# Gated mix of a spectral filter and a Mish MLP: the order of the input loads, and a new written-out order of all engine queues

## The chip, the cores and the metric

The kernel runs on 1 core of one Trainium2 chip. The metric is the device time of one execution in microseconds (us), the slowest core's, as a median over runs. The profile shows one execution, with times counted from its first instruction.

## The reference, cut to what matters

```python
x = A_x                                                   # [1, 2048, 512] bf16
g = sigmoid((x * gate_w).sum(-1, keepdims=True))
# A: 2-D real FFT over tokens and features, times a complex weight, back
X = rfft2(x.astype(f32), axes=(-2, -1)) * (w_r + 1j * w_i)   # w: [2048, 257]
a = irfft2(X, s=(2048, 512)).astype(bf16)
# B: MLP with Mish, F = 1792
h = einsum("bsd,df->bsf", x, w1) + b1
act = h * tanh(log1p(exp(-abs(h))) + max(h, 0))
b = einsum("bsf,fd->bsd", act, w2)
return g * a + (1 - g) * b
```

Both branches read the same x. Branch A is a chain of small matmuls against constant tables with two passes through memory in between; branch B is two large matmuls.

## The kernel before, in words

Tokens are tiled as 16 tiles t of 128 partitions (token = 16 * partition + t); features are 4 slices of 128, the 1792 hidden units 14 slices "ft". B handles the tokens in 4 chunks c of 512.

**Names of the tasks.** Each piece of work is a named task, and the names below are used throughout.

- Loads, all but a few on the queue of SyncE (SP): `ld_x0` to `ld_x12` (x by groups of tiles, lines 433 to 435), `ld_w1_lo_h` (w1 by ranges of ft and halves of the features, 437 to 441), `ld_fm`, `ld_gm`, `ld_rf`, `ld_ri` (tables of the transforms), `ld_gw`, `ld_b1`, `ld_Wp..`, `ld_Wm..`, `ld_Wz.` (18 loads of the spectral weight W, 458 to 463), `ld_w2_0`, `ld_w2_1`.
- x transposed: tiles 0 to 7 through TensorE (`tr`, line 481) and copied out of PSUM (`evx`, 409/410); tiles 8 to 15 by VectorE in 32 x 32 blocks (`tp8` to `tp15`, line 489) and then by 16 shuffle DMAs (`sh`, line 495), half of them on SP's queue and half on GpSimd's. A shuffle waits for all eight `tp`.
- B: `mm1_c_ft` (line 795, four matmuls of 512 columns), `mish_c_ft` on ScalarE (811), `mm2_t_part` (830, seven matmuls of 512 columns), `bev_t` (776/777, scaled by 1 - g into xo).
- A, forward: `ts`, `td` (sums and differences, VectorE, 414), `a10_t`, `a11_t` (533), `eg_t` (ScalarE, 540), `e1p`, `e1m`, `e1f` (VectorE, 414, 549/550), `s1_t` (559), `e2_t` (564), `r1w` (scratch written: 16 DMAs on SP, 568) and `r1r0` to `r1r3` (scratch read back, 640).
- A, spectrum, in four groups v: `s2_u` (656), on VectorE `wm` (times W, 414, PSUM to Qb), on GpSimd `wz` (414, Qb to Zb), the small chain `cv`, `crv`, `rcc`, `cv2`, `cm`, `chs`, `wc` for one column, then `s2i_v` (716), `e4` (copies out), `r2w_v` (scratch written, 726), and after all four `r2r0` to `r2r3` (731). Before the first product stand `wcols`, `rcw`, `weff`, `wab1`, `wab2`, which need all 18 loads of W.
- A, inverse, by tile: `s1i_t` (744), `e5_t`, `a1i_t` (755), `gc_t` (ScalarE, 760), `sam_t`, `sap_t` (VectorE, 766), `sbm_t`, `sbp_t` (GpSimd, 414; for tiles 14 and 15 also on VectorE), then `sum_t` (VectorE, 414, 850) and the stores `out`; tiles 14 and 15 end in `fin` (842).
- Gate: `gdot` (16 on VectorE, 575), `gpow` (GpSimd, 580), `gadd`, `gcol`, `omg` (582 to 585).

**The order.** It is not found at build time. A string `ORDER` lists every task of the program in one sequence: two digits (base 62) are the number of the task in the order in which the code adds them, then comes the engine where there is a choice, and the PSUM bank where the task opens one.

```python
for _ in tasks:                                            # lines 230 to 251, shortened
    t = tasks[digit(2)]
    if t.opts:
        t.eng, t.dur, t.fn = next(o[:3] for o in t.opts if o[0] == ENGINE[ORDER[pos]])
    for p in t.alloc or ():
        b0 = digit(1)
        ...                                                # waits for the last users of the bank
    order[t.eng].append(t)
```

Each engine runs its own list strictly in this order and waits, in front of a task, for what the task reads, for the buffer it overwrites and for its bank. A wait holds everything behind it on that engine; SP's list holds DMA issues alone. The loads themselves are added here:

```python
433  def ld_x(t0, t1):
434      dma(f"ld_x{t0}", xo[:, t0:t1, :], xv[:, t0:t1, :], ...)
...
451  ld_x(8, 12)
452  ld_w1(8, 14, ("sp", "sp"))
453  ld_x(12, 16)
```

**SP's list of before, decoded:** ld_x0, x2, fm, w1_4_0, x4, x8, w1_8_0, w1_8_1, x12, gm, gw, Wp00; eight `sh`; w2_1 and nine loads of W; r1w0b; Wm01, w2_0, Wp13, Wp11; then `r1w` with Wp03 and Wm11 among them; Wp01, Wm13, rf; r1r0, r1r3, r1r1, r1r2; ri; r2w0 to 3; r2r0 to 3; the stores. GpSimd's list has `ld_b1` and the other eight `sh`.

**VectorE's list of before** in the front: evx0a, 0b, 2a, 2b, ts0, td0, ev_small, e1m_2, evx6, tp10, tp9, evx4, tp11, 8, 13, 14, 15, 12, ts1, e1p_2, e1p_0, td1, e1m_0, then `gdot` among `e1`; the last nine `gdot` behind e2_12, gadd, gcol, omg, weff, then wm01, cv_1, wm00.

Of the kernel before, what the change touches and what calls it, by code (L numbers as in the profile page):

```python
# [257 lines left out]
ORDER = (
    "0M04005060P070208090A000B0Q0C010R0D0E0F0G0H0T0I0x60J0N0yv0K0z50L7510V0O7F211610v13312v7K47A714v767L0S7M770U787"
    "B0W7C1Zv7G1X0037H1av1l50X1b61n1m33J0Y1Y0Z1pv7D7P00a17518v1d1B791A7T67U15116v1C191E7R51c60b1F1G7I7Q1D7N1Q7f01N1"  # L260
    "vv7J7h11V7b21ov1ev1wv7O1U1S7V41W7g7c8307E7S8J21fv1J1M8977i1P8H534283332718K1O1T1L36841y20v1x01gv0g0j1K7W381z0i"
    "8L41I0l8D68701R8M7z4297x18820v2Bv1H2Av8A21v350c2Iv2Ca2Hv7X02Jv8E22a7d32fv2D60s807y0f7Y0p2iv2gv7e2Kv1h10o2L41qv"
    "8l02N1iv0k2M32Ea1k8B48510e2Pv0u2V22W60q8n70m2hv8C2F2Ov8m2X861j0h2Yv2Zv1r30n1sa2Qa8b02312k62j32G8F42av8I24v262t"
    "52l1u2u38o2b12v2mv2nv1t2xv8177v52ca2R125822d2wv2ya2z68G372oa2e8p32Sv7w2p4392qv3A7Z130a8t68r22U3C8N73E8Z47a318u"
    "8h52T3B8q8a2r8c3G8x33D3F2s320d8j13H3I0r3K3L0t8k3T7s68f48O3O7t3W3P03M3N3Q8s8i3U3X18g3R8Pa3hv3S3Y47j77p07ua3a7q3"
    "gv3lv8d63kv3jg8y3Z3b7k8e7rv3t23ig3u43ng43v3V3v4F07la7m63mg8z74H903w42v47v3x46v7n3c79P24Ov4G37oa44g3y63d9X50w45"
    "g49g3e9Q4I4Sv9Y8v23z8w4J8Q748g4Pv4Tv4K28R4L403f3o3p34b08Sv8T23rv4M419T74A3qa9U8U4B34N4d4Rg8Va3s4kv4Qg4lv4Da4c0"
    "4Vg4W9V74Ca4e4Ug4mg4pv4f9W4E8W24ov4ng4g44h4i9N34qg4X49F04j4Za9114Yv9O4rg4s4t4924uv4va4a9Z49D38X9459G9J64w9L79E"
    "9M9709a8Ya93a954x5915H35Aa5P751496v5Qa9b29K5R55S4y9c5v15f75n65Iv5J352v5U5K5B4985T5wa4z5325C5M5L5oa5D5Wg5Vg5E5x"
    "55Ng5gv5y605Og9R15z5p350545X699a9H45Ya6R75q5Fg566J65Gg5h09S6Ka556Sv62gA1v5r9d56B16T29e61g5s5i9A76x66L36U5k6Ca6"  # L270
    "V6D55ug5Z15j6309I6EA8v58g57g5a5tgA2v6M5mg6p46W9B9yv5lg6N6Yg6ya6qa6h26ia6O9f66z2A7v5c6G5b706Xg5dg64aA5v719i45eg"
    "650A36Z36Pg6F6r59l1669Ca6Ig6j79zv6s9g6Qg6aa6b39j9m729p267689s0AEv6k6HgA4v6Ag74v6u6c6t9v5A96l69g6mA06wvA6ABv6d9"
    "ka6eAAv6vv6ogAC9haADv6ng9nAHv6fg73g6ggAF9o9qAGv9rAI9t9w9u9x"
)
# [17 lines left out]
def _build(nc, A_x, A_w_r, A_w_i, B_x, B_w1, B_b1, B_w2, gate_w, out):  # L292
# [8 lines left out]
    with es:  # L301
# [76 lines left out]
        def dma(name, dst, src, reads=(), writes=(), nbytes=0, deps=(), is_out=False, prio=None, queue="sp", bw=380e3, tail=1.1, nd=128, issue=0.62):  # L378
            t = G.add(name, queue, issue if issue != 0.62 or queue != "pool" else 1.0, lambda e: e.dma_start(dst, src),  # L379
                      reads=reads, writes=writes, lat=tail, deps=deps, prio=prio)  # L380
# [584 lines left out]
```

## Time and profile before

| what | value |
|---|---|
| runs, median (lowest to highest of 3) | 131.43 us (130.37 to 131.91) |
| the profiled execution's own time | 131.48 us |
| its span, first to last instruction | 129.7 us |
| busy: TensorE / VectorE / ScalarE / GpSimd | 123.0 / 91.6 / 69.4 / 56.3 us |
| granted TensorE clock | 1.00 |

A row of the timeline gives the start, the busy time of the merged instructions, engine, line, operation, out<-in, their count, and in brackets the idle time before them with what ended it. "PE" is TensorE, "PEld" its weight loads, "DVE" VectorE, "ACT" ScalarE, "POOL" GpSimd; a "q" behind it is the engine's sequencer, which issues DMAs. A busy time of several pipelined matmuls runs over into the next row by some 0.16 us.

### The profile page before, as it was taken

The numbers are of one execution on the slowest core, as the hardware profiler recorded it, in microseconds if no ns is written. First come the engines' busy times: TensorE is split into PE (matmuls) and PEld (weight loads), VectorE is DVE, ScalarE is ACT, GpSimd is POOL, SyncE is SP. The second block draws the span as 40 slices with busy tenths as digits, with TensorE's granted clock in tenths as the row PEclk, the third lists the DMA queues.
The fourth block names the chain that finished last, engine by engine and source line by source line (L and its number), as shares of the span: only waits on it lengthen the run. The fifth ranks groups of instructions, "written<-read, shape, count | busy, mean of one in ns | idle before, by whom it ended". The sixth has DMA issues, their size and how long they took to land.

```text
span 129.7 us, 2726 instructions
## 1 busy us (share of the span) xinstructions
PE 123.0 (95%) x1014; PEld 66.1 (51%) x1014; DVE 91.6 (71%) x178; ACT 69.4 (54%) x119; POOL 56.3 (43%) x90
## 2 busy tenths in 40 slices
PE   7999999999999999699999999999999999999960
PEld 5776546445554444344444444444447666555650
DVE  0456999898699981179499795541006997999992
ACT  1306777798997537500336047454077988674300
POOL 4000047000000009146879499930000799979770
PEclk9999999999999999999999999999999999999999
DMA  3999618799998667991000032555089000224045
GB/s 88 337 402 394 199 40 219 216 263 189 289 314 242 197 173 223 331 390 43 0 5 3 0 93 73 162 162 159 13 285 356 3 5 3 81 81 157 10 152 172
DMA packets 19293, 21.16 MB, mean 163 GB/s; under 512 B 1744, under 2 KB 15952, under 8 KB 19152
## 3 DMA queue, kind: packets, MB, share of 16 engines
q1 hardware_dynamic: 18176, 19.67, 48.6%
q10 hardware_dynamic: 816, 0.79, 1.9%
q0 software_dynamic: 288, 0.53, 1.5%
q8 instruction: 8, 0.13, 0.4%
q14 instruction: 5, 0.04, 0.1%
HBM read 13.64 MB, written 6.29 MB: 154 GB/s over the span
## 4 chain that ended last, share of the span: by engine, by line
PE 85%; DMA 5%; DVE 3%; POOL 2%; issue 1%; POOLq 1%; DVEq 0%
PE ps L795 37%; PE ps L830 29%; DMA Abuf<-scr 5%; PE ps L744 3%; PE ps L755 3%; PE ps L533 3%; PE ps L559 3%; PE ps L430 3%; POOL Tg L414 2%; PE ps L656 2%; PE ps L716 2%; DVE Qb L766 1%; PE ps L481 1%; DVE xo L842 1%; DVE xT L409 1%
## 5 line engine op out<-in xcount | busy, mean ns | idle before, releaser
L795 PE MATMUL ps<-xT,w_sb 128*128 128x512 bf16 (+1 forms) x240 | 53.8, 365 | 0.3 <-DVE xT L409 0.3
L830 PE MATMUL ps<-w_sb,act 128*128 128x512 bf16 (+2 forms) x252 | 52.2, 355 | 0.0
L811 ACT ACTIVATE act<-ps,b1f 128x512 bf16<-128x512 f32 x56 | 36.5, 687 | 26.6 <-PE ps L795 26.6
L830 PEld LDWEIGHTS ps<-w_sb,act 128*128 128x128 bf16 x252 | 22.8, 98 | 23.0 <-issue 0.6
L795 PEld LDWEIGHTS ps<-xT,w_sb 128*128 128x128 bf16 x240 | 22.3, 98 | 21.9 <-DVE xT L409 0.8
L414 POOL TENSOR_TENSOR Tg<-Qb 128x256 bf16<-128x256 f32 x29 | 22.6, 812 | 17.4 <-DVE Qb L766 17.4
L414 POOL TENSOR_TENSOR Zb<-Qb 128x510 bf16<-128x510 f32 x16 | 20.0, 1268 | 3.2 <-DVE Qb L414 2.6
L414 DVE TENSOR_TENSOR Qb<-ps,WT 128x1024 f32<-128x1024 f32 x16 | 18.9, 1215 | 3.4 <-PE ps L656 3.3
L766 DVE SCALAR_TENSOR_TENSOR Qb<-ps,gcol,Qb 128x256 f32<-128x256 f32 x32 | 13.6, 473 | 1.5 <-issue 0.8
L580 POOL TENSOR_TENSOR gcol<-omg,gdot 128x16 f32<-128x16 f32 x1 | 2.9, 2942 | 26.6 <-DVE Tg L575 26.6
L410 ACT ACTIVATE Ybuf<-ps 128x1024 bf16<-128x1024 f32 x9 | 9.1, 1024 | 6.5 <-PE ps L716 6.2
L414 DVE TENSOR_TENSOR Abuf<-ps,Tg 128x512 bf16<-128x512 f32 x16 | 10.4, 685 | 2.7 <-ACT Tg L540 1.5
L409 DVE CAST Ybuf<-ps 128x1024 bf16<-128x1024 f32 x7 | 8.6, 1223 | 3.8 <-PE ps L716 3.1
L379 POOL DMA_DIRECT2D xT<-act x8 | 4.0, 503 | 15.5 <-DVE act L489 15.5
L575 DVE SCALAR_TENSOR_TENSOR Tg<-xo,Tg 128x512 bf16<-128x512 bf16 x16 | 10.5, 685 | 0.2
L776 ACT ACTIVATE xo<-ps,omg 128x512 bf16<-128x512 f32 x11 | 7.3, 687 | 5.2 <-PE ps L830 3.5
L777 DVE TENSOR_SCALAR xo<-ps,omg 128x512 bf16<-128x512 f32 x3 | 2.3, 751 | 10.8 <-PE ps L830 10.8
L760 ACT ACTIVATE Qb<-ps,gcol 128x256 f32<-128x256 f32 x16 | 7.1, 473 | 4.3 <-PE ps L755 4.2
L414 DVE TENSOR_TENSOR xo<-xo,Tg 128x512 bf16<-128x512 bf16 x14 | 9.0, 653 | 0.0
L540 ACT ACTIVATE Tg<-ps 128x512 f32<-128x512 f32 x8 | 4.7, 594 | 6.2 <-PE ps L533 6.2
L410 ACT ACTIVATE Zb<-ps 128x512 bf16<-128x512 f32 x12 | 7.0, 603 | 1.0 <-PE ps L744 1.0
L409 DVE COPY xT<-ps 128x512 bf16<-128x512 bf16 (+1 forms) x6 | 2.9, 505 | 5.7 <-PE ps L481 5.7
(61 smaller groups left out, 88.1 us busy)
## 6 DMA issues: line engine op xcount, KB each, us to landing
Abuf<-scr SPq DMA_DIRECT2D x8, 512.0 KB, 6.8
scr<-Ybuf SPq DMA_DIRECT2D x16, 128.0 KB, 2.2
scr<-Ybuf SPq DMA_DIRECT2D x4, 512.0 KB, 2.9
w_sb<-in_B_w_dram SPq DMA_DIRECT2D x2, 896.0 KB, 6.6
out_dram<-xo SPq DMA_DIRECT2D x7, 256.0 KB, 2.0
xo<-in_A_x_dram SPq DMA_DIRECT2D x3, 512.0 KB, 7.5
rt<-c_rt SPq DMA_DIRECT2D x2, 512.0 KB, 7.4
WT<-in_A_w_r_dram SPq DMA_DIRECT2D x7, 128.5 KB, 5.6
```

Of the source, the lines that this page charges most:

```text
L379: t = G.add(name, queue, issue if issue != 0.62 or queue != "pool" else 1.0, lambda e: e.dma_start(dst, src), reads=reads, writes=writes, ...
L409: fs = {"dve": ("dve", dve_dur(n, rate=rate), lambda e: e.tensor_copy(out=dst(), in_=src())), "act": ("act", act_dur(n), lambda e: e.activ ...
L410: "act": ("act", act_dur(n), lambda e: e.activation(dst(), src(), AF.Copy))}
L414: f = lambda e: e.tensor_tensor(out=o(), in0=i0(), in1=i1(), op=op)
L540: G.add(f"eg_{t}", "act", act_dur(512), lambda e, gb=gb, pa=pas[0], pv=pv: e.activation(G0[:, gb].rearrange("p t c (m s) -> p t c m s", s= ...
L575: lambda e, t=t: e.scalar_tensor_tensor(out=junk[t % 2], in0=xo[:, t, :], scalar=1.0, in1=gwb, op0=ALU.mult, op1=ALU.mult, accum_out=gdot[ ...
L760: lambda e, t=t, sl=sl, p5=p5: e.activation(gC[:, sl, :].rearrange("p (i n) -> p i n", i=2), ps[:, p5.bank, :].rearrange("p (i n) -> p i n ...
L766: lambda e, t=t, sl=sl, p5=p5, o=o, op=op: e.scalar_tensor_tensor(out=st1[:, sl, o::2, :], in0=ps[:, p5.bank, :].rearrange("p (i n) -> p i ...
L776: G.add_multi(f"bev_{t}", [("act", act_dur(512, True), lambda e: e.activation(xo[:, t, :], ps[:, pd.bank, :], AF.Copy, scale=omg[:, t:t + ...
L795: ins = e.matmul(o if c < 2 else o.rearrange("p (a t j) -> p a t j", a=4, t=4), w1_sb[:, i, 128 * ft:128 * (ft + 1)], xTp[:, i, 512 * c + ...
L811: lambda e, c=c, ft=ft, pd=pd, hb=hb: e.activation(act[:, hb, ft, :].rearrange("p (t a j) -> p t a j", t=4, a=4), ps[:, pd.bank, :].rearra ...
L830: ins = e.matmul(ps[:, pd.bank, cs_], act[:, hb, ft, 128 * tl:128 * (tl + 1)], w2_sb[:, ft, cs_], start=(ft == 0), stop=(ft == NFT - 1))
```

## The change

Two lines of the loads change places, so x's tiles 12 to 15 are issued in front of w1's last slices (ft 8 to 13), and the string `ORDER` is replaced as a whole. No task is added or removed; 23 copies, scalings and sums change their engine (21 between ScalarE and VectorE, in both directions, and two between GpSimd and VectorE), and many tasks change their PSUM bank.

```diff
@@ -256,21 +256,21 @@
 ORDER = (
-    "0M04005060P070208090A000B0Q0C010R0D0E0F0G0H0T0I0x60J0N0yv0K0z50L7510V0O7F211610v13312v7K47A714v767L0S7M770U787"
...
+    "0M0N0420506070P080O090A0B0U0C00010Q0D0R0E020F0G0H0I0x00yv0J0K0L0T0z30S10v037F27511151347A314v1X67K70V7B12a1Y7G"
...
@@ -449,8 +449,8 @@
         ld_x(8, 12)
+        ld_x(12, 16)
         ld_w1(8, 14, ("sp", "sp"))
-        ld_x(12, 16)
```

What the new string says, decoded:

| list | new order, where it differs |
|---|---|
| SP | ld_x0, x2, fm, w1_4_0, x4, x8, **x12, w1_8_0, w1_8_1**, Wp00, **Wm00**, gw, gm; eight `sh`; Wp01, Wm10, **w2_1**, Wz0, Wm13, Wz1, Wm11, Wm12, Wm02, Wm03, **w2_0**, Wp11, Wp12, Wp03; r1w0b, Wp13, Wp10, then the other fifteen `r1w` without a load among them; Wp02, Wm01, rf; r1r and all behind it as before, the stores in another order |
| GpSimd | ld_b1 first; then ones, ident, ebz; the eight `sh`; ebase behind them. Then wz01, **wz00**, crv_0, wz11, **cm_0, chs_0**, wz10, **wc0**, ... and the `sb` in the order 2, 0, 1, 3, 4, 5, 6, 7, ... 12, 13, 14 |
| VectorE | evx0a, 0b, 2b (**evx2a on ScalarE**), ts0, td0, ev_small, e1m_2, **e1p_2, evx4, evx6, tp8, 9, 10, 13, 15, 12, 11, 14**, ts1, td1, gdot0, ...; the last eight `gdot` behind e2_12, then **weff, gadd, cv_0, wm01, gcol, wm00, wm10, omg**, bev_3, cv_1, wm11, cv2_0, ... |
| TensorE, to the first `s2` | both lists have the same length of work in front; rcw stands one `mm2` half earlier |
| TensorE, first `s2` to first `s1i` | 15 `mm2` halves and 15 `mm1` (before: 17 and 13); up to s2i_3 10 and 10 (before: 12 and 9), behind it 5 and 5 (before: 5 and 4) |
| TensorE, behind the first `s1i` | 11 `mm2` halves and 2 `mm1` (before: 9 and 4), then tile 15 as before; behind the last `a1i` three `mm2` halves (before: two) and tile 15 |

Of the 18 loads of W one stood in front of the shuffles before and two do now; the inverse table (`ld_ri`) stands behind the shuffles, and behind r1r2, in both lists.

More of the change, by code (lines that the diff above doesn't have):

```diff
@@ L258 @@
 ORDER = (
-    "0M04005060P070208090A000B0Q0C010R0D0E0F0G0H0T0I0x60J0N0yv0K0z50L7510V0O7F211610v13312v7K47A714v767L0S7M770U787"
[L260 to L273, printed above, removed]
+    "0M0N0420506070P080O090A0B0U0C00010Q0D0R0E020F0G0H0I0x00yv0J0K0L0T0z30S10v037F27511151347A314v1X67K70V7B12a1Y7G"
@@ new lines @@
+    "7C7L0W7M7H761Zv1av7D1l41m01n7I0X7R51c60Y7E1547J1pv1ov173777T216v7818v0b0c7S191A7V00a791B1b31E1G8350Z7U1D1C1d1F"
+    "7v41vv7N1M1V1K8L17P27O1T7w1L1wv1H7W893337f71W2741N1O1fv348F07Q841R8G1U1qa0d8D236292857g381ev2Av7b03A8J47c1P8M0"
+    "l7x71x61y07h10v1J8K1z1Q1gv2Bv351S1I20v0j21v2Cv2iv0r8B47y2fv0s8H52Hv8E7i2Iv2Jv8A2D08l61h20n0p2Ea2L72V07d18I2Kv8"
+    "m2gv1r50g2N2X0i1iv0u0m22v0o0h2M22hv1sa8C2W38578702351k2Pv2u42Yv0q2Zv0k7e2t32Ov1j1t2k124v2G2aa2j2861u2F7z72b52v"
+    "2wv2xv2l2Qa88252R22ca8n0802ya8d4262e2z52nv2Sv2U2mv3C8e2oa8Z7372p22T2qv2d30a3J8a7X17Z68r731328j48x58t23E2s7Y398"
@@ new lines @@
+    "f38u8p18y7a8b28o3B3G2r0f7s50e3D7j08s8c7t3I3F0t3H3K3O8h63P77k3Q3R8k3S8q3L3T3Y18g3X33W3Z3U3hv8i3M3gv7p73kv8v67q3"
+    "jg8133N7uv8w3ig823a7m47la3b3lv3V3c63ng3t24F03d3e3u542v0w3f3mg7n3o3v7ra43v45g3w8N746v8O7oa3x44g47v48g3y249g3p33"
+    "z4H4Ov9Z28Pa8Q73ra4Pv4Qg4G03qa4b34Tv4I4Rg9a9R54J9D69N29S404d9E4K54Sv9X08R4lv414L4A4kv4c54Ug9O9Y4Vg4e4B04M8Sa4C"
+    "a4N9P44f4pv8W74W4ov8z54g64mg4ng4Da4X04h8T64rg3s904Zv4qg4i4j9J54s4Ya4t04E9Q4ua8U4vv4a9H49V09T19F28Va943959K9W9I"
+    "9d68X4w4x96a9U9e9154y9G5905135H45Ia4z505P29L65J15Aa5n45K5Qv52v5M5L5R25oa5B09M8Yv533925X45C5v7545S5Ya56555f19A6"
@@ L274 @@
+    "5Z49b35ga5p15Ng5E5Og5U93a5a57g5D5T5wa5q58g6J56305h264a5Fg5Vg6B75b6Ka5i5c5s5dgA1v9B5Wg5Gg6h45r5x05eg6L56Cv9yv6Z"
+    "19c6535k665j68679Ca9zv5y9i76D25mg6R66E6x35tg5z6M5lg60A2v61g9j62g6av6Sa6p06iaA5v6T66G9ka6U9f46b15ug9776FA0A4v6N"
+    "6Ag6j26ya6c6V986z36qaA7v6r09g6Ig6W6O9l69m9p569g6Hg6Qg6e6Yg6d6Pg6k99a6s9s19v76l6mAAvA8vABvADvAC6gg6t6XgA9706fg6"
+    "u71A3AEv6ogAF726wv73v9ha6vg6ng74v9nAHvAGv9q9t9wA69oAI9r9u9x"
 )
```

## The prediction

> **What bounds the kernel now.** I read the head of the page first, then the busy time by stretches, the chain of waits, and last the queues of the engines one by one.
>
> ```profile
> span 129.7 us, 2726 instructions
> PE 123.0 (95%) x1014; PEld 66.1 (51%) x1014; DVE 91.6 (71%) x178; ACT 69.4 (54%) x119; POOL 56.3 (43%) x90
> ```
>
> ```profile
> 17.50:48.00 30.50, 30.50 (x178) 15.31 (x177) 28.07 (x64) 24.05 (x43) 3.96 (x8) 1.00 0.86 225
> 48.00:55.30 7.30, 6.09 (x31) 2.74 (x28) 1.31 (x7) 4.43 (x7) 3.99 (x6) 1.00 0.87 267
> 55.30:86.10 30.80, 30.79 (x357) 13.87 (x361) 23.36 (x32) 11.29 (x16) 24.14 (x39) 1.00 0.23 81
> 86.10:97.70 11.60, 11.60 (x85) 5.39 (x85) 1.23 (x1) 4.71 (x7) 0.00 (x0) 1.00 0.57 181
> 97.70:129.70 32.00, 27.65 (x250) 17.76 (x248) 27.83 (x58) 18.07 (x37) 22.63 (x29) 1.00 0.27 98
> ```
>
> The columns behind each length are PE, PEld, DVE, ACT and POOL busy, clock, DMA share and GB/s. TensorE is full in three of the five stretches. Its work is the same in the changed kernel, so a new order can win only where TensorE waits or where the end is not its own. There are two such places: 1.2 us in 48.00:55.30, and the end.
>
> ```profile
> PE ps L656 <- DMA Abuf<-scr: 1.2, 1, 1.2
> ```
>
> ```profile
> 48.40 6.87 DMA Abuf<-scr
> 119.32 1.66 DVE Qb L766 x4
> 121.05 1.71 POOL Tg L414 x2
> 126.75 0.52 DVE xo L842 x2
> ```
>
> The wait is for r1r0, issued at 48.40 and landed 6.87 us later, at 55.27. The end (from the chain in order of time) runs from the inverse's last products over GpSimd and VectorE to `fin`, not over TensorE.
>
> ```profile
> 55.31 0.63 PE L656 MATMUL ps<-Abuf,rt 64*32 64x256 bf16 x32 [1.23 <-DMA Abuf<-scr]
> 86.06 0.64 PE L716 MATMUL ps<-Zb,rt 32*64 32x256 bf16 x32
> 97.65 1.06 PE L744 MATMUL ps<-GMs,Abuf 128*128 128x128 bf16 x16
> 119.10 6.28 PE L830 MATMUL ps<-w_sb,act 128*128 128x512 bf16 x56
> ```
>
> From TensorE's timeline: the first s2 at 55.31, the last s2i at 86.06, the first s1i at 97.65, and from 119.10 the last mm2, which end near 125.3. VectorE ends at 126.75 + 0.52 = 127.27; the last store and the rest take 2.43 us more. So the end hangs over TensorE's by about 2 us.
>
> **Step 1, x's last tiles in front of w1's last pieces: nothing by itself.**
>
> ```profile
> 4.19 1.23 SPq L379 DMA_DIRECT2D w_sb<-in_B_w_dram  x2
> w_sb<-in_B_w_dram SPq DMA_DIRECT2D x2, 384.0 KB, 8.3
> xo<-in_A_x_dram SPq DMA_DIRECT2D x1, 512.0 KB, 9.6
> 10.16 0.69 DVE L414 TENSOR_TENSOR Abuf<-ps,Tg 128x512 bf16<-128x512 f32 x1 [1.07 <-PE ps L795]
> 13.84 3.70 DVE L489 STREAM_TRANSPOSE act<-xo 128x512 bf16<-128x512 bf16 x6
> ```
>
> The w1 pieces were issued from 4.19 and landed by 5.42 - 0.6 + 8.3 = 13.1; x12, issued behind them at 5.46, at 15.06. The last six transposes ran without a wait from 13.84 to 17.54, so VectorE's queue, not x's landing, set their end. Now x12 lands about 2 us earlier, which nobody needs, and the w1 pieces end where x12 ended, near 15.0. Their first user was mm1_0_12 at 13.6; the new string puts mm1_1_13 first, at 15.6 by the sum of the matmuls ahead of it. Cost 0 with a cover of about 0.6 us; without the cover it is what they come later, one for one.
>
> What does move is VectorE's queue ahead of the transposes. e1m_2 began at 10.16. In the new list TensorE reaches a10_2 0.4 us earlier (two small matmuls fewer ahead of it), then come e1m_2, e1p_2, evx4, evx6 and all eight transposes back to back: 9.7 + 2 x 0.61 + 2 x 0.6 + 8 x 0.61 = 17.0. Both evx and the two e1 are paid anyway; evx2a goes to ScalarE, which is idle there. Gain 0.5 us, with bounds 0 (evx4 waits for tr4) and 0.7; I take 0.4: the shuffles start at 17.15.
>
> **Step 2, SP's queue: r1r0 goes out earlier.**
>
> ```profile
> 17.57 5.02 SPq L379 DMA_DIRECT2D xT<-act  x8
> 47.23 0.60 SPq L379 DMA_DIRECT2D rt<-c_rt  x1
> 48.40 2.43 SPq L379 DMA_DIRECT2D Abuf<-scr  x4
> ```
>
> From the first shuffle at 17.57 to the end of rf's issue at 47.83 SP issued 44 DMAs almost without a hole: 30.26 / 44 = 0.69 us each, and then 0.57 us of waits in front of r1r0. So r1r0 is set by the number of issues, not by the data. Now 43 stand between (Wm00 went in front of the shuffles): 17.15 + 43 x 0.69 + 0.57 = 47.4, one us earlier. Every r1w still has its e2 ahead of it in my walk; the closest is r1w8b, reached at 38.0 to 38.5, whose e2_8 ends at 37.2 (VectorE's list: e2_4 ends 34.3, three e1 of 0.61, 1.15 for itself). The same loads lie in the DMA queue in front (two of W, and rf), so the 6.87 us stay: r1r0 lands at 54.2. TensorE arrives by its own work at 53.9, since both lists are equally long up to here. Gain 1.1 us, bounds 0 (an issue stalls in the queue) and 1.4 (TensorE itself).
>
> The W loads still end behind the r1w: Wm01 lands near 48.8, wcols follows, and rcw at 52.4 keeps 3 us of cover. omg now stands behind wm10, so 1 - g comes near 59 in place of 52. Behind it wait bev_3 on VectorE and bev_0, bev_2 on ScalarE, and for those s2_4, due at 61.4; bev_0 ends at 60.9. Cost 0, one for one if that 0.5 us is gone.
>
> **Step 3, the spectrum: less cover over a chain on GpSimd.**
>
> ```profile
> 60.58 0.86 PE ps L795 x4
> 61.45 1.51 PE ps L830 x7
> 58.31 1.26 POOL L414 TENSOR_TENSOR Zb<-Qb 128x510 bf16<-128x510 f32 x1 [1.64 <-DVE Qb L414]
> 85.31 0.23 POOL L703 TENSOR_TENSOR Zb<-ch 128x8 bf16<-128x8 f32 x1
> L414 POOL TENSOR_TENSOR Zb<-Qb 128x510 bf16<-128x510 f32 x16 | 20.0, 1268 | 3.2 <-DVE Qb L414 2.6 <-PE ps L716 0.6
> ```
>
> An mm1 is 0.86 us, an mm2 half 1.51. From the first s2 to s2i_3 there were 12 halves and 9 mm1, now 10 and 10: 2 x 1.51 - 0.86 = 2.16 us less, so 30.75 becomes 28.6 and s2i_3 is reached at 54.2 + 28.6 = 82.8. GpSimd's chain took from 58.31 to 85.54, 27.2 us, for at most the 24.14 us that the whole stretch shows busy; begun 3.0 us behind the first s2 as before, it would end at 54.2 + 3.0 + 27.2 = 84.4, 1.6 us too late. But its holes were waits for VectorE's products and for cv2, and the new list has these earlier (cm_0 at the sixth place of the chain, before at the tenth). Walking the new lists with 1.15 us for a wm and 1.25 for a wz: wz01 starts at 57.8 (behind wm01 and wm00), wz11 at 61.0 (behind wm11), wz21 at 64.0, wz40 at 69.2, wz60 at 76.3 (behind s2i_1), and wc3 ends at 81.9; no hole is over 0.7 us. Bounds of the stall: 0 and 1.6; I take 0, since the work alone (57.8 + 24.1 = 81.9) is on that side too, with 0.9 us to spare.
>
> Behind s2i_3 there are now 5 halves and 5 mm1 (before 5 and 4), 11.9 us to the first s1i with s2i_3 itself 12.4.
>
> ```profile
> Abuf<-scr SPq DMA_DIRECT2D x1, 512.0 KB, 4.0
> 93.08 1.76 SPq L379 DMA_DIRECT2D Abuf<-scr  x4
> ```
>
> The road through memory took from 86.06 to 93.08 + 4.0 = 97.1, 11.0 us, so r2r0 has 1.4 us of cover where it had 0.6. The first s1i comes at 82.8 + 12.4 = 95.2, or 97.65 - 1.1 (step 2) - 1.3 (2 halves fewer, 2 mm1 more) = 95.25.
>
> **Step 4, the tail.** TensorE has 11 halves and 2 mm1 left in place of 9 and 4, 1.3 us more: its end is 125.3 - 1.1 = 124.2 and goes no lower. VectorE's work behind the first s1i is the same but for which tiles it takes: 27.83 us busy in the window row, four copies, one bev, 32 products, 14 sums, three sb and four fin.
>
> ```profile
> 97.86 0.75 DVE L777 TENSOR_SCALAR xo<-ps,omg 128x512 bf16<-128x512 f32 x1 [9.85 <-PE ps L830]
> 98.53 1.28 DVE L409 CAST Zb<-ps 128x512 bf16<-128x512 f32 x2
> 121.22 0.95 DVE L414 TENSOR_TENSOR xo<-xo,Tg 128x512 bf16<-128x512 bf16 x1
> 126.34 0.41 DVE L414 TENSOR_TENSOR xo<-xo,Tg 128x512 bf16<-128x512 bf16 x1
> L414 DVE TENSOR_TENSOR xo<-xo,Tg 128x512 bf16<-128x512 bf16 x14 | 9.0, 653 | 0.0
> L414 DVE TENSOR_TENSOR Tg<-Qb 128x256 bf16<-128x256 f32 x3 | 2.3, 765 | 0.0
> ```
>
> The copies came 0.9 us behind the first s1i (98.53). So 95.25 + 0.95 + 27.83 and holes of about 1.1 us (before, from the bev at 97.86: 127.27 - 97.86 - 27.83 = 1.6) give 125.1; bounds 124.6 (TensorE's end and one fin) and 126.5 (a1i_14 is now followed by 1.5 us more of mm2, so the last products no longer end the chain, but the holes may be 2.5). With 2.43 behind it: 127.5, against 129.7.
>
> **The sum:** -1.1 (r1r0) and -1.1 (the overhang at the end) make -2.2 on the profiled execution's 131.48, which is 0.05 above the median of the runs: **129.3 us**.
>
> **The rivals.**
>
> *A, GpSimd's chain keeps its length.* If the spectrum takes 27.2 us behind the first wz as before, s2i_3 waits 1.6 us, and all behind it slides: 130.9. For it: its holes came out of round trips over three engines, which a list on paper shortens easily. Against: there are only 3.1 us of holes in the 27.2 to begin with, and half of them would have to come back in other places.
>
> *B, r1r0 is no earlier.*
>
> ```profile
> 32.27 2.31 SPq L379 DMA_DIRECT2D WT<-in_A_w_i_dram  x2
> ```
>
> Two issues in the old SP list took 2.31 us where others take 1.3, and more of that kind may fall into the new one; then only the tail is left, and that begins 1.1 us later: 130.4.
>
> *C, slower: the sums meet a busy GpSimd.* A sum took 0.41 us at 126.34, when GpSimd had ended, and 0.95 at 121.22, beside a GpSimd product; 14 took 9.0. In the new list GpSimd starts at 98.7 and works almost to the end, and five sums stand close together before its last products. If all 14 take 0.95 and the three sb as much, that is 13.3 + 2.9 - 9.0 - 2.3 = 4.9 us more, and the end 129.3 + 4.9 = 134.2. It decides the sign from 2.2 us on, the case of over 1% slower from 3.5. Against: most of the old ones were slowed already (mean 0.65), and the last two sums and all three sb now come behind GpSimd's end. The Trainium skill (SBUF — State Buffer, Who interferes with whom) says that a VectorE instruction with two inputs in SBUF contends with a GpSimd instruction that reads SBUF, and that the loser blocks fully; by that rule a sum is either 0.41 or waits out a GpSimd product. The rows 0.41 and 0.95 agree with it.
>
> *D, a chain of small stalls in the front.* Several banks are taken over with 0.1 to 0.3 us to spare; if TensorE loses 3.5 us there by one engine being late, it is slower too: 132.9.
>
> *E, nothing at all:* the change of the loads alone does not move the end, as in step 1, and if gain and loss cancel it stays at 131.4.
>
> **How the numbers follow.** The forecast gets 0.56, A 0.12, B 0.09, C 0.11, D 0.05, E 0.07. The forecast's own range is 128.3 (TensorE's end sets it, and a run low by 0.3) to 130.1. A measurement of this kernel tells about 1% (1.3 us) from no change. Faster by over 1% (under 130.1): the forecast and a little of B, 0.58. Slower by over 1%: C and D, 0.16. Within: the rest, 0.26. The range 128.1 to 132.2 leaves out C, D and a little below.
>
> **What would show it.** Right: the first r1r issued near 47.4 and s2 at 54.2 with a wait under 0.4; s2i_3 near 82.8 and the first s1i near 95.2 without waits on TensorE; TensorE's last matmul near 124.2 and the last fin within 1 us of it. Wrong: PE waiting for Zb in front of L716 (A), SP's 43 issues taking over 30 us (B), sums of 0.8 us and more on the mean (C), PE's waits of over 1 us before 54 (D).

## The result, and the profile after

The changed kernel takes **129.59 us** (median of 20 runs, 129.19 to 130.91) against 131.20 us for the kernel before (20 runs between them on the same chip, 130.37 to 132.48): a ratio of **0.9892, 95% interval 0.9866 to 0.9918**, so 1.1% faster. The profiled execution took 129.91 us, where that of before took 131.48. The forecast was 129.3. The ratios here and below leave out executions that took over 1.5% longer than the fastest of the same kernel; the medians do not.

The first line of the page after, its line of the chain by engine, and three of its groups (busy, mean ns, idle before and what ended it):

```profile
span 128.2 us, 2701 instructions
...
PE 82%; DVE 13%; issue 2%; DVEq 0%; ACT 0%
...
L766 DVE SCALAR_TENSOR_TENSOR Qb<-ps,gcol,Qb 128x256 f32<-128x256 f32 x32 | 13.7, 474 | 1.7 <-ACT Qb L760 1.5
...
L414 DVE TENSOR_TENSOR xo<-xo,Tg 128x512 bf16<-128x512 bf16 x14 | 8.7, 644 | 0.0
...
Abuf<-scr SPq DMA_DIRECT2D x8, 512.0 KB, 6.6
```

The span is 1.5 us shorter. No DMA stands in the chain any more; VectorE holds 13% of it, and that part is the tail. TensorE's timeline after, at the places that the prediction named:

```profile
16.38 3.40 PE L795 MATMUL ps<-xT,w_sb 128*128 128x512 bf16 x15 [0.35 <-issue]
...
54.69 0.63 PE L656 MATMUL ps<-Abuf,rt 64*32 64x256 bf16 x32
...
83.09 0.64 PE L716 MATMUL ps<-Zb,rt 32*64 32x256 bf16 x32
95.55 1.06 PE L744 MATMUL ps<-GMs,Abuf 128*128 128x128 bf16 x16
...
116.51 7.79 PE L830 MATMUL ps<-w_sb,act 128*128 128x512 bf16 x62
```

The 1.23 us in front of the first `s2` are gone, and there is no wait in front of s2i_3 (83.09) or of the first `s1i` (95.55). A small new one stands at 16.38. TensorE ends at 116.51 + 7.79 = 124.30. VectorE's timeline after, the transposes and the end:

```profile
12.50 4.85 DVE L489 STREAM_TRANSPOSE act<-xo 128x512 bf16<-128x512 bf16 x8
...
96.65 1.29 DVE L409 CAST Zb<-ps 128x512 bf16<-128x512 f32 x2 [11.61 <-PE ps L744]
...
110.83 0.41 DVE L414 TENSOR_TENSOR xo<-xo,Tg 128x512 bf16<-128x512 bf16 x1
...
116.64 3.23 DVE L414 TENSOR_TENSOR xo<-xo,Tg 128x512 bf16<-128x512 bf16 x4
...
121.74 1.76 DVE L414 TENSOR_TENSOR Tg<-Qb 128x256 bf16<-128x256 f32 x3
...
124.08 0.74 DVE L414 TENSOR_TENSOR xo<-xo,Tg 128x512 bf16<-128x512 bf16 x2
124.74 0.99 DVE L842 SCALAR_TENSOR_TENSOR xo<-ps,omg,Tg 128x256 bf16<-128x256 f32 x3
```

VectorE ends at 124.74 + 0.99 = 125.73, still 1.4 us behind TensorE (before: about 2). So the span falls into four pieces, and each can be compared:

| kernel | first s2 | from there to the first s1i | from there to VectorE's end | behind it |
|---|---|---|---|---|
| before | 55.31 | 42.34 | 29.62 | 2.43 |
| changed | 54.69 | 40.86 | 30.18 | 2.47 |
| difference | -0.62 | -1.48 | +0.56 | +0.04 |
| forecast | -1.1 | -1.3 | +0.2 | 0 |

The sum is -1.50 us of span, where -2.2 was forecast. The middle pays for the whole change; the front gave half of what was expected, and the tail took some back.

### The profile page after: what moved, and what is told of

Its sections match the earlier page's. It is cut to its first block, busy times and chain, and to the rows that moved or that the text cites. A ratio compares the mean times of both kernels' runs of the same rounds, so it can differ in the third digit from the quotient of the medians.

```text
span 128.2 us, 2701 instructions
## 1 busy us (share of the span) xinstructions
PE 122.0 (95%) x998; PEld 66.6 (52%) x1014; DVE 88.3 (69%) x175; ACT 71.4 (56%) x122; POOL 56.5 (44%) x90
## 4 chain that ended last, share of the span: by engine, by line
PE 82%; DVE 13%; issue 2%; DVEq 0%; ACT 0%
PE ps L795 38%; PE ps L830 26%; DVE Qb L766 5%; DVE xo L414 5%; PE ps L430 3%; PE ps L533 3%; PE ps L559 3%; PE ps L744 2%; PE ps L716 2%; PE ps L481 2%; PE ps L755 2%; PE ps L656 2%; DVE Tg L414 1%; DVE xo L842 1%; DVE Zb L409 0%
## 5 line engine op out<-in xcount | busy, mean ns | idle before, releaser
L795 PE MATMUL ps<-xT,w_sb 128*128 128x512 bf16 (+1 forms) x237 | 53.0, 366 | 0.6 <-issue 0.3
L830 PE MATMUL ps<-w_sb,act 128*128 128x512 bf16 (+2 forms) x240 | 49.8, 354 | 0.8 <-issue 0.3
L811 ACT ACTIVATE act<-ps,b1f 128x512 bf16<-128x512 f32 x56 | 35.8, 690 | 21.0 <-PE ps L795 16.7
L766 DVE SCALAR_TENSOR_TENSOR Qb<-ps,gcol,Qb 128x256 f32<-128x256 f32 x32 | 13.7, 474 | 1.7 <-ACT Qb L760 1.5
L776 ACT ACTIVATE xo<-ps,omg 128x512 bf16<-128x512 f32 x12 | 8.1, 686 | 11.0 <-PE ps L830 8.5
L410 ACT ACTIVATE Ybuf<-ps 128x1024 bf16<-128x1024 f32 x10 | 10.0, 1021 | 2.2 <-PE ps L716 1.7
L409 DVE CAST Zb<-ps 128x512 bf16<-128x512 f32 x4 | 2.6, 680 | 11.6 <-PE ps L744 11.6
L409 DVE CAST Ybuf<-ps 128x1024 bf16<-128x1024 f32 x6 | 7.3, 1221 | 2.8 <-PE ps L716 2.2
## 6 DMA issues: line engine op xcount, KB each, us to landing
scr<-Ybuf SPq DMA_DIRECT2D x16, 128.0 KB, 3.8
WT<-in_A_w_r_dram SPq DMA_DIRECT2D x7, 128.5 KB, 6.8
```

The lines of the kernel that those rows point to most:

```text
L409: fs = {"dve": ("dve", dve_dur(n, rate=rate), lambda e: e.tensor_copy(out=dst(), in_=src())), "act": ("act", act_dur(n), lambda e: e.activ ...
L410: "act": ("act", act_dur(n), lambda e: e.activation(dst(), src(), AF.Copy))}
L766: lambda e, t=t, sl=sl, p5=p5, o=o, op=op: e.scalar_tensor_tensor(out=st1[:, sl, o::2, :], in0=ps[:, p5.bank, :].rearrange("p (i n) -> p i ...
L776: G.add_multi(f"bev_{t}", [("act", act_dur(512, True), lambda e: e.activation(xo[:, t, :], ps[:, pd.bank, :], AF.Copy, scale=omg[:, t:t + ...
L795: ins = e.matmul(o if c < 2 else o.rearrange("p (a t j) -> p a t j", a=4, t=4), w1_sb[:, i, 128 * ft:128 * (ft + 1)], xTp[:, i, 512 * c + ...
L811: lambda e, c=c, ft=ft, pd=pd, hb=hb: e.activation(act[:, hb, ft, :].rearrange("p (t a j) -> p t a j", t=4, a=4), ps[:, pd.bank, :].rearra ...
```

## The experiments

All are compared with the kernel before, run alongside them (medians 131.0, 131.2 and 131.3 us). "Against the changed kernel" is the quotient of two such ratios. The last three columns are pieces as in the table above, the last of them called the tail.

| experiment | ratio to before, 95% | first s2 | s2 to s1i | s1i to VectorE's end |
|---|---|---|---|---|
| changed, old place of x12 | 0.9974, 0.9938 to 1.0010 | 55.74 | 40.86 | 30.18 |
| before, new place of x12 | 1.0077, 1.0038 to 1.0117 | 55.59 | 42.34 | 29.61 |
| changed, inverse one piece later | 1.0012, 0.9979 to 1.0045 | 54.19 | 42.37 | 29.97 |
| before, Wm00 and Wm02 earlier | 1.0011, 0.9979 to 1.0042 | 55.02 | 42.47 | 29.63 |
| before, Wp01 and Wm13 earlier | 0.9953, 0.9927 to 0.9979 | 54.28 | 42.34 | 29.63 |
| changed, Wp02 and Wm01 earlier | 0.9876, 0.9840 to 0.9912 | 54.11 | 40.87 | 30.19 |
| changed, tail rearranged | 0.9992, 0.9958 to 1.0025 | 54.70 | 40.87 | 31.50 |
| changed, mm1_1_13 later | 0.9869, 0.9835 to 0.9903 | 54.60 | 40.87 | 30.18 |
| changed, four sums later | 0.9938, 0.9909 to 0.9967 | 54.79 | 40.86 | 30.80 |
| changed, W's two and mm1_1_13 | 0.9843, 0.9821 to 0.9865 | 54.35 | 40.87 | 30.18 |
| the last two in one | 0.9932, 0.9911 to 0.9953 | 54.88 | 40.86 | 30.80 |

Each list keeps its own distances where the edit lies elsewhere: 42.34 to 42.47 and 29.6 with the old string, 40.86 and 30.18 with the new one, so to 0.13 us or less. What an edit does to one piece passes on to the end, in full or, for the inverse, all but 0.2 us.

### The change of the loads, undone and alone

```diff
 SP of the changed kernel: ... x4, x8,
-    x12, w1_8_0, w1_8_1, Wp00, ...
+    w1_8_0, w1_8_1, x12, Wp00, ...
```

> The changed kernel with one thing undone: x12 is issued behind w1's last two pieces again; all lists are otherwise the new ones. Theory T (the end hangs on the start of the spectrum, and that on SP's queue behind the shuffles): in the new list all evx come first and tp13 is due at 14.3, so x12 landing near 16.0 holds VectorE, the shuffles start 0.7 to 1.7 us later (18.1 to 19.1 in place of 17.38), r1r0 lands as much later, and the time rises by 0.5 to 1.5 us over the changed kernel. Rival R (the load swap is worth nothing by itself, as step 1 of the prediction had it): no change, or 0.35 us faster, because TensorE's wait for w1's last piece at 16.03 goes.

Measured 130.47 us, 0.8% slower than the changed kernel. VectorE's timeline of this run, and then TensorE's:

```profile
12.04 1.89 DVE L489 STREAM_TRANSPOSE act<-xo 128x512 bf16<-128x512 bf16 x3
15.79 3.08 DVE L489 STREAM_TRANSPOSE act<-xo 128x512 bf16<-128x512 bf16 x5 [1.87 <-DMA xo<-in_A_x_dram]
```

```profile
20.11 0.40 PE L533 MATMUL ps<-FMs,Tg 128*128 128x128 bf16 x4 [1.08 <-DVE Tg L414]
...
55.74 0.63 PE L656 MATMUL ps<-Abuf,rt 64*32 64x256 bf16 x32 [0.38 <-DMA Abuf<-scr]
```

The new order of VectorE reaches tile 13's transpose at 13.9 and waits 1.87 us for x12; the shuffles go out 1.52 us later than in the changed kernel (18.90) and r1r0 0.79 us later (48.72). TensorE stands 1.08 us in front of `a10_6`, which needs VectorE's work behind the transposes, and s2 is 1.05 us late. So the two parts of the change need each other: the pulled-up transposes are worth nothing without x12 in front.

```diff
 SP of the kernel before: ... x4, x8,
-    w1_8_0, w1_8_1, x12, gm, ...
+    x12, w1_8_0, w1_8_1, gm, ...
```

> The kernel before with one thing done: x12 issued in front of w1's last two pieces; all lists are otherwise the old ones. Theory T: the old TensorE list uses w1's last pieces at 13.6, so TensorE waits there 1.4 to 2.4 us; of this the 1.2 us wait for r1r0 gives some back, and the time rises by 0.3 to 1.2 us over the kernel before. The shuffles do not move (VectorE's list sets them). Rival R (the earlier x is where the gain of the change comes from): 0.5 to 1.6 us faster than before.

Measured 131.89 us, 0.8% slower than the kernel before. TensorE's timeline of this run:

```profile
14.85 7.07 PE L795 MATMUL ps<-xT,w_sb 128*128 128x512 bf16 x32 [0.62 <-issue]
...
55.59 0.63 PE L656 MATMUL ps<-Abuf,rt 64*32 64x256 bf16 x32 [0.73 <-DMA Abuf<-scr]
```

With the old string the first user of w1's last pieces comes at 14.2, before they land, and TensorE stands 0.62 us (1.4 to 2.4 were expected). That delay goes on to e2_0 and so to r1w0b on SP's queue (31.01 where it was 30.24). The swap alone costs, though this profile shows only a part of the 0.8%: its VectorE ends at 127.54, 0.27 us behind that of the kernel before. With the new string the wait for w1's last piece was 0.35 us in the changed kernel's profile (16.38); in the other profiles with x12 in its new place and the same TensorE list it lay between nothing and 0.60.

### The place of the inverse

```diff
 TensorE of the changed kernel: ... mm2_7_1, mm2_8_0,
-    s1i_1, s1i_0, s1i_2, s1i_3, mm1_3_4, a1i_2, ..., mm2_8_1, s1i_4
+    mm2_8_1, s1i_1, s1i_0, s1i_2, s1i_3, mm1_3_4, a1i_2, ..., s1i_4
```

> The changed kernel with one mm2 half (mm2_8_1) moved from behind a1i_0 to in front of the first s1i, so the first inverse matmuls come 1.5 us later and TensorE's total work and end stay. Theory T (VectorE's chain from the first s1i sets the end): the first s1i at 97.0, the first sam at 99.8, the end 0.5 to 1.5 us later than the changed kernel (not all of 1.5, since VectorE's later holes close). Rival R (TensorE's own work sets the end and the pulled-forward inverse is not what pays): within 0.3 us of the changed kernel.

Measured 131.13 us, 1.2% slower than the changed kernel. TensorE's timeline:

```profile
96.56 1.06 PE L744 MATMUL ps<-GMs,Abuf 128*128 128x128 bf16 x16
```

The distance from s2 to s1i grows from 40.86 to 42.37, which is one half of an `mm2` (1.51), and the tail keeps all but 0.2 of it. That is the size of the change's whole gain. So the gain in the middle is the position of the inverse among the `mm2`: VectorE's chain begins earlier, and work that it need not wait for goes behind. Two halves fewer and two `mm1` more in front of it are 1.30 us by their lengths; where the other 0.18 us of the 1.48 come from was not traced.

### SP's queue: which issues set r1r0

```diff
 SP of the kernel before:
-    ..., Wp00, 8 x sh, w2_1, ..., Wm00, ..., Wm02, ..., r1w0b, ...
+    ..., Wp00, Wm00, Wm02, 8 x sh, w2_1, ..., r1w0b, ...
```

> The kernel before with two loads of W (Wm00 and Wm02) moved in SP's list from behind the shuffles to in front of them, nothing else. Theory T (r1r0's issue is set by the number of SP issues behind the shuffles): the first r1r goes out 1.2 to 1.4 us earlier, near 47.1, r1r0 lands near 54.0, the first s2 starts at 54.0 and the time falls by 0.9 to 1.3 us. Rival R (r1r0's landing is set by the amount of data in the DMA queues, or the end does not hang on the spectrum's start): within 0.3 us of before.

Measured 130.98 us, no change. SP's queue and VectorE's copy e2_0 in the kernel before, and then SP's queue in this run:

```profile
30.24 0.69 SPq L379 DMA_DIRECT2D scr<-Ybuf  x1
```

```profile
28.98 1.22 DVE L409 CAST Ybuf<-ps 128x1024 bf16<-128x1024 f32 x1
```

```profile
26.54 1.90 SPq L379 DMA_DIRECT2D WT<-in_A_w_i_dram  x3
30.27 0.69 SPq L379 DMA_DIRECT2D scr<-Ybuf  x1
...
48.22 2.07 SPq L379 DMA_DIRECT2D Abuf<-scr  x4
```

SP issued nothing from 28.44 to 30.27: it stood in front of r1w0b, which needs e2_0. In the kernel before e2_0 ended at 30.20 and r1w0b went out at 30.24, after a wait of 0.28 us. Two issues fewer in front of that wait are worth nothing; r1r0 goes out 0.18 us earlier and not the 1.3 of two issues.

```diff
 SP of the kernel before:
-    ..., Wp00, 8 x sh, ..., 13 x r1w, Wp01, Wm13, rf, r1r0, ...
+    ..., Wp00, Wp01, Wm13, 8 x sh, ..., 13 x r1w, rf, r1r0, ...
```

> The kernel before with the last two loads of W (Wp01 and Wm13, the ones right in front of rf and r1r0) moved in front of the shuffles. The two of the earlier try stood ahead of r1w0b, where SP waits for e2_0's data at 30.27 anyway. Theory T2 (r1r0 is set by the issues between r1w0b and r1r0, not by all behind the shuffles): the first r1r goes out 0.9 to 1.3 us earlier (47.1 to 47.5), r1r0 lands near 53.5, TensorE's own work then sets the first s2 (54.0), and the time falls by 0.9 to 1.3 us. Rival R (the end does not hang on the spectrum's start): within 0.3 us of before.

Measured 130.41 us, 0.5% faster than the kernel before (interval 0.2 to 0.7%). SP's queue, and TensorE's timeline:

```profile
45.46 0.60 SPq L379 DMA_DIRECT2D rt<-c_rt  x1
47.04 2.03 SPq L379 DMA_DIRECT2D Abuf<-scr  x4
```

```profile
54.28 0.63 PE L656 MATMUL ps<-Abuf,rt 64*32 64x256 bf16 x32
```

Two issues again, this time taken from behind r1w0b, move r1r0 by 1.36 us (48.40 to 47.04) although the shuffles start 0.23 us later here, and TensorE no longer waits for it. The gain is less than the 0.9 to 1.3 us expected, though in the profile VectorE's end moved by 1.02 us (127.27 to 126.25). (Between rf's end at 46.06 and r1r0 stand 0.98 us where there were 0.57, so the next limit, presumably the last r1w's landing, is near.) So in the kernel before the count that matters is that of the issues behind r1w0b. There are 24 of them, and 20 in the changed kernel. By 0.66 us each that is -2.6 us, but r1w0b itself goes out later in the changed kernel, at 32.38 instead of 30.24 (+2.1), because fourteen loads stand between the shuffles and it, one of them a long one of 1.45 us. (Before there are eleven: w2_1 and ten loads of W, not nine as the list of before has it.) The difference, -0.5, is what r1r0 gained (48.40 to 47.93).

```diff
 SP of the changed kernel:
-    ..., Wp00, Wm00, gw, gm, 8 x sh, ..., 15 x r1w, Wp02, Wm01, rf, r1r0, ...
+    ..., Wp00, Wm00, Wp02, Wm01, gw, gm, 8 x sh, ..., 15 x r1w, rf, r1r0, ...
```

> The changed kernel with the two loads of W right in front of rf (Wp02 and Wm01) moved in front of the shuffles. Theory T2 (in the new lists TensorE's own work reaches the first s2 no earlier than r1r0 lands, so the front's limit has passed to TensorE): r1r0 lands 1 us or more earlier, the first s2 stays within 0.3 us, and the time is within 0.3 us of the changed kernel. Rival (SP's queue still sets it): 0.5 us or more faster than the changed kernel.

Measured 129.62 us, within 0.2% of the changed kernel. SP's queue and TensorE's timeline:

```profile
46.52 2.08 SPq L379 DMA_DIRECT2D Abuf<-scr  x4
```

```profile
54.11 0.63 PE L656 MATMUL ps<-Abuf,rt 64*32 64x256 bf16 x32
```

r1r0 goes out 1.41 us earlier, and s2 starts without a wait. It is 0.58 us earlier, more than the 0.3 expected: TensorE's transposes began 0.32 us earlier in this execution, and there was no wait for w1's last piece. This front no longer hangs on SP: TensorE's own work sets it, so the last 1.4 us on SP's queue buy little.

```diff
 TensorE of the changed kernel:
-    ..., mm1_1_13, ..., mm1_1_7, ...
+    ..., mm1_1_7, mm1_1_13, ...
```

> The changed kernel with mm1_1_13, the first user of w1's last pieces, moved behind mm1_0_4 and mm1_1_7, 1.7 us later. Theory T2 (the wait of 0.35 us at 16.03 was for w1's last piece, landed at 16.07 behind x12, and TensorE sets the front): the wait goes and the time falls by 0 to 0.35 us, more where the piece lands later. Rival (the front has room): no change within 0.2 us.

Measured 129.42 us, 0.2% under the changed kernel, which the intervals do not tell from nothing. TensorE's timeline:

```profile
14.12 5.56 PE L795 MATMUL ps<-xT,w_sb 128*128 128x512 bf16 x25
```

The matmuls run through where the changed kernel stood for 0.35 us: that wait was for w1's last piece. s2 came at 54.60, only 0.09 earlier, partly because this execution began later: the way from the third group of transposes (the row of eight L481 matmuls) to s2 is 0.16 shorter. Of the other 0.19 us, 0.13 lie in that group itself, which took 0.74 us here and 0.61 in the changed kernel.

### The tail

```diff
 changed kernel, behind the first s1i
 ScalarE: + bev_7 (in front of e5_2), + e5_12 (behind e5_13); gc_3, gc_1, gc_0 in front of mish_3_4
 VectorE: - bev_7, - e5_12
-   sam_2, sap_2, sam_0, sap_0, sam_1, sam_3, sap_1, sap_3, sap_4, ...
+   sam_2, sap_2, sam_3, sap_3, sam_1, sap_1, sam_0, sap_0, sum_2, sap_4, ...
 GpSimd:
-   sbm_2, sbp_2, sbm_0, sbp_0, sbm_1, sbm_3, sbm_4, sbp_3, ...
+   sbm_2, sbp_2, sbm_3, sbp_3, sbm_1, sbp_1, sbm_0, sbp_0, sbm_4, ...
```

> The changed kernel with VectorE relieved in the inverse: bev_7 and e5_12 go to ScalarE (bev_7 into its idle time ahead of the first s1i), gc_3, gc_1 and gc_0 come earlier on ScalarE, and the sa and sum are put in that order, so VectorE has two pieces of work (1.3 us) and the holes behind the first sam less. TensorE's list is the same. Theory T (VectorE's chain from the first s1i sets the end, TensorE's end is 1.1 to 1.4 us ahead of it): 0.5 to 1.1 us faster than the changed kernel. Rival (GpSimd's row of products, full from 110 to 122.9, sets it): within 0.3 us.

Measured 131.09 us, 1.0% slower than the changed kernel. VectorE's timeline:

```profile
105.13 1.27 DVE L766 SCALAR_TENSOR_TENSOR Qb<-ps,gcol,Qb 128x256 f32<-128x256 f32 x3 [2.77 <-POOL Tg L414]
```

The edit was a bad test: tiles 0 and 4 share one buffer for the products, and with tile 0 last on GpSimd VectorE waited 2.77 us to write tile 4. Work of 1.3 us had been taken off VectorE, a hole of 2.77 came in, and the tail grew by 1.32 (30.18 to 31.50). It does not tell VectorE's chain from GpSimd's row, the rival, since GpSimd too ended 1.35 us later (124.22 for 122.87). What the relief alone is worth is left open.

```diff
 VectorE of the changed kernel:
-   ..., sum_8, sum_7, sum_9, sum_10, sap_14, sam_14, sap_15, sum_11, sam_15, sbp_14, sbm_15, sbp_15,
-   fin_14_1, sum_13, sum_12, fin_15_0, ...
+   ..., sap_14, sam_14, sap_15, sam_15, sbp_14, sbm_15, sbp_15, sum_8, sum_7,
+   fin_14_1, sum_9, sum_10, sum_11, sum_13, sum_12, fin_15_0, ...
 SP: the stores in the order in which the sums end
```

> The changed kernel with sum_8, sum_7, sum_9 and sum_10 moved on VectorE's list from in front of the last four products (sap_14, sam_14, sap_15, sam_15) to behind the three sb of tiles 14 and 15, and SP's stores put in the order in which the sums now end. In the changed kernel these four sums took 0.81 us each beside a GpSimd that worked without a hole until 122.87; a sum behind that end took 0.37. Theory T (a sum's length is set by whether a GpSimd product runs beside it, and VectorE's chain sets the end): the sums that now fall behind GpSimd's end take 0.37 to 0.41 us, those still beside it 0.6 to 0.95; two or three of them fall behind it, VectorE's end moves from 125.7 to 125.1 to 125.4 and the time by -0.3 to -0.6 us. Rival L (the length hangs on something else, such as the tile or the place in VectorE's queue): the four still take 0.8 each, the end stays at 125.7 and the time within 0.1 us of the changed kernel's. Rival P (TensorE's end is the bound already): sums shorter, time the same.

Measured 130.67 us, 0.5% slower than the changed kernel. The group of the sums on this run's page, VectorE's timeline, and GpSimd's last row:

```profile
L414 DVE TENSOR_TENSOR xo<-xo,Tg 128x512 bf16<-128x512 bf16 x14 | 6.8, 511 | 0.0
```

```profile
117.91 0.88 DVE L766 SCALAR_TENSOR_TENSOR Qb<-ps,gcol,Qb 128x256 f32<-128x256 f32 x2 [1.09 <-ACT Qb L760]
119.25 0.88 DVE L766 SCALAR_TENSOR_TENSOR Qb<-ps,gcol,Qb 128x256 f32<-128x256 f32 x2 [0.47 <-POOL Tg L414]
120.04 2.49 DVE L414 TENSOR_TENSOR Tg<-Qb 128x256 bf16<-128x256 f32 x3
...
123.78 1.75 DVE L414 TENSOR_TENSOR xo<-xo,Tg 128x512 bf16<-128x512 bf16 x5
```

```profile
110.15 12.10 POOL L414 TENSOR_TENSOR Tg<-Qb 128x256 bf16<-128x256 f32 x16 [0.28 <-DVE Qb L766]
```

The mechanism is there: GpSimd ended at 122.25, and five sums behind that took 1.75 us, 0.35 each, where four beside it took 0.81 each in the changed kernel; all 14 fell from 8.7 to 6.8 us. But the time went the wrong way. The sums had filled the 1.09 and 0.47 us in which VectorE now waits for ScalarE and for a buffer, and the three sb, now beside GpSimd to their end, took 2.49 instead of 1.76. Saved 1.9, paid 1.56 and 0.73: that is 0.4 of the 0.62 us by which the tail is longer; the rest is spread too thin to name. GpSimd's row ended 0.7 us earlier behind the first s1i than in the changed kernel, and VectorE's end came 0.62 us later: so VectorE's chain sets the end, and not GpSimd's row.

### The front's edits together, and with the tail's

The first kernel has W's two loads in front of the shuffles and mm1_1_13 later; the second has the four sums behind the products as well.

> The changed kernel with the last two loads of W (Wp02, Wm01) in front of the shuffles, as in the experiment that moved them alone, and mm1_1_13 behind mm1_1_7, as in the experiment that moved it alone. Theory T (with W's loads moved r1r0 lands before TensorE needs it, and TensorE's own front, with 0.35 us of waiting for w1's last piece, sets the first s2): the two edits add up now though each alone gave little; s2 starts at 53.7 to 53.8 (54.69 in the changed kernel, 54.11 with the loads alone), the first s1i at 94.6 to 94.8, the time is 0.8 to 1.0 us below the changed kernel's, 128.6 to 128.9. Rival R (r1r0 still sets it): s2 at 54.1 as with the loads alone, and 0.3 to 0.5 us below the changed kernel.

> The two other kernels of this call in one: W's two loads in front of the shuffles, mm1_1_13 later, and the four sums behind the products. Theory T (front and tail are two separate terms): the gains add, s2 at 53.7 to 53.8, VectorE's end at 124.1 to 124.5, the time 1.1 to 1.6 us below the changed kernel's, about 128.0 to 128.5. Rival P (the tail is bound by TensorE, so that the sums' move brings nothing more): the same time as with the front's edits alone, 128.6 to 128.9.

Measured 129.34 us (ratio to before 0.9843) and 130.44 us (0.9932). The first is the best kernel of the study, 0.5% under the changed one, with two intervals that only just do not meet. Its s2 came at 54.35, not at the forecast 53.7: the run with W's loads alone already had no wait at w1, so there was nothing left for the second edit to add in the profile. The second shows the loss of the sums' move again (its tail is 30.80, as with that move alone). The two forecasts of an added gain, 128.6 to 128.9 and 128.0 to 128.5, both failed. TensorE's timeline of the first, then of the second:

```profile
5.55 0.61 PE L795 MATMUL ps<-xT,w_sb 128*128 128x256 bf16 x4
6.00 0.61 PE L481 MATMUL ps<-ident,xo 128*128 128x128 bf16 x8
...
54.35 0.63 PE L656 MATMUL ps<-Abuf,rt 64*32 64x256 bf16 x32
```

```profile
5.63 1.02 PE L795 MATMUL ps<-xT,w_sb 128*128 128x256 bf16 x4
6.49 0.61 PE L481 MATMUL ps<-ident,xo 128*128 128x128 bf16 x8
...
54.88 0.63 PE L656 MATMUL ps<-Abuf,rt 64*32 64x256 bf16 x32
```

Both have the same front. From the third group of transposes to s2 they take 48.35 and 48.39 us, so the half microsecond between their s2 arose before 6.5 us.

## Why the prediction was right, and where its steps were off

**What bounded the kernel** was read rightly: TensorE full in the middle, a wait for r1r0, and an end that is VectorE's. The forecast was 0.3 us from the median, in part by luck: it was reckoned from the profiled execution's 131.48 us, and the median of before came out at 131.20. Its -2.2 us of span became -1.50; the profiled execution fell by 1.57, the medians by 1.6.

**Step 1** priced the swap of the loads at nothing, since "x12 lands about 2 us earlier, which nobody needs". That sentence is wrong for the new string: without the swap VectorE waits 1.87 us (first experiment, 0.8%). The step had computed eight transposes back to back and had not asked when the fourth needs x12. The cover for w1's pieces was wrong too: they landed later than 15.0, and TensorE stood 0.35 us (0.60 and 0.51 in two of the other profiles) where a cover of 0.6 had been claimed. The shuffles began at 17.38 against the forecast 17.15.

**Step 2** forecast r1r0's issue at 47.4 and s2 at 54.2. SP's queue after:

```profile
17.38 5.06 SPq L379 DMA_DIRECT2D xT<-act  x8
...
29.62 2.08 SPq L379 DMA_DIRECT2D WT<-in_A_w_i_dram  x2
31.75 0.59 SPq L379 DMA_DIRECT2D WT<-in_A_w_r_dram  x1
32.38 0.68 SPq L379 DMA_DIRECT2D scr<-Ybuf  x1
33.10 1.24 SPq L379 DMA_DIRECT2D WT<-in_A_w_i_dram  x2
34.38 11.01 SPq L379 DMA_DIRECT2D scr<-Ybuf  x15
...
46.76 0.60 SPq L379 DMA_DIRECT2D rt<-c_rt  x1
47.93 1.79 SPq L379 DMA_DIRECT2D Abuf<-scr  x4
```

The 43 issues took 29.98 us to 47.36, 0.70 each, as forecast within 0.3; two long ones (in the rows of 2.08 for two, and of 11.01 for fifteen) make the difference. With the shuffles' 0.23 that is 47.93, and r1r0 landed 6.6 us later at 54.53. The number came out near in part by luck. The step's rule, that all issues behind the shuffles count, was read off the kernel before, and there it fails: issues in front of r1w0b end in a wait for e2_0, as the experiment on Wm00 and Wm02 shows. In the changed kernel the rule fits, because SP has no wait there (the load in front of r1w0b ended at 31.75 + 0.59, and r1w0b went out at 32.38): three loads more and a long one fill that time, and four issues fewer stand behind it. The step had not asked whether the queue waits. The lower bound was wrong as well: TensorE was to be there at 53.9, and came at 54.6 to 54.7 (0.35 for w1, the rest from its start, below). The two arrive together, so the gain was 0.62 and not 1.1.

**Step 3** held. GpSimd's timeline after:

```profile
58.01 2.49 POOL L414 TENSOR_TENSOR Zb<-Qb 128x510 bf16<-128x510 f32 x2 [2.19 <-DVE Qb L414]
...
82.41 0.23 POOL L703 TENSOR_TENSOR Zb<-ch 128x8 bf16<-128x8 f32 x1
...
110.05 12.82 POOL L414 TENSOR_TENSOR Tg<-Qb 128x256 bf16<-128x256 f32 x16 [0.28 <-DVE Qb L766]
```

The chain took 58.01 to 82.64, 24.6 us, where it had been 27.2, and ended 0.45 us ahead of s2i_3 at 83.09 (forecast: 57.8, 81.9 and 82.8). s2 to s2i_3 was 28.40 us for 28.6, and from there to s1i 12.46 for 12.4. Rival A did not come. The delayed inverse cost 1.51 us of distance, so what the inverse's place is worth is shown by experiment, too; that GpSimd's new order keeps s2i_3 from waiting is read from this one profile.

**Step 4** forecast the tail from s1i to VectorE's end at 29.9 us; it was 30.18. The busy time by stretches after (PE, PEld, DVE, ACT, POOL, as before):

```profile
95.60:128.20 32.60, 28.49 (x252) 18.34 (x254) 27.36 (x58) 17.11 (x35) 22.47 (x29) 1.00 0.26 96
```

The first copy came 1.10 behind s1i (0.95 forecast), VectorE was busy for 27.36 (27.83), and its holes, most of them on ScalarE's `gc` as the row of L766 says, were the remaining 1.72 (1.1). Only the holes were mis-sized by more than half a microsecond. TensorE's end was 124.3 for 124.2, which is luck in part: s2 came 0.5 us later than forecast, and from there to its end TensorE took 69.61 us where it had taken 70.07, which the step had put as equal.

**Rival C**, the sums beside a busy GpSimd, did not come: 14 took 8.7 us, 0.3 less than before. Sums are longer beside a working GpSimd, 0.81 for four of them and 0.37 behind its end, but as a group they were no longer than before. The Trainium skill (SBUF — State Buffer, Who interferes with whom) has VectorE instructions with two inputs in SBUF contend with GpSimd's reads, and the loser blocked fully; sums of 0.35 to 0.37 and of 0.81 agree. Not every sum in GpSimd's busy time was held up, as the 0.41 at 110.83 shows, and why not was not tested. Rivals B and D left small traces: two long issues, and one stall of 0.35.

## What to carry to other kernels

Split the span at two or three instructions that both kernels have, and compare distances, not times: here each list kept its own to 0.13 us or less wherever the edit lay elsewhere, and an edit's effect is read in the piece where it lies. When an issue queue sets a landing, look for the last wait in that queue and count only what stands behind it; all issues count only where there is no wait. An instruction that fills a wait costs nothing there, so moving it elsewhere gains nothing, even if it gets shorter. An earlier start for one engine pays only if the load in front of it comes earlier too.

## What the runs showed of the hardware

**The start of TensorE differed between profiles by up to 0.9 us with the same list.** The third group of transposes began between 5.58 and 6.49 in the nine kernels with the same TensorE list up to s2 (but for the place of mm1_1_13). The way from it to s2 was 48.35 to 48.64 in six of them, the upper end being the changed kernel's with its 0.35 of waiting, 48.90 and 49.07 in the two with 0.60 and 0.51 of waiting for w1, and 50.16 with x12 in its old place. In the rows above the four matmuls in front of the group took 0.45 us in one execution (5.55 to 6.00) and 0.86 in the other (5.63 to 6.49). The Trainium skill (TensorE: Matmul & The Clock Gate, What's actually happening) says that the clock opens by a free-running window, so that the moment differs by about half a microsecond either way; these rows agree in size, but the profile gives the granted clock as 1.00 in both, so no run here shows that cause. Some of the difference is x's landing: three of the nine profiles have a wait of 0.16 to 0.26 us for it in front of the first transposes. With one profile for each kernel it also stays open whether the start changes from execution to execution or stays with a kernel: the medians of the last two kernels differ by 1.10 us, where their tails give 0.62. A difference of half a microsecond ahead of 6.5 us should not be put down to an edit that lies behind it.

**An issue on SP's queue is dear and uneven.** From the shuffles to r1r0 0.57 to 0.70 us is the rule, but in each of the thirteen profiles one or two issues take 1.0 to 1.9 us, of other tasks in different executions: the two loads of W in the row at 29.62 took 2.08, and two in the row at 33.10 took 1.24. All of these began between 29.2 and 33.8 us or between 36.4 and 39.2. What lengthens them was not tested.
